# First two weight quads by plain block products, the whole beginning issued from one listed order

## The chip, the cores and the metric

One core of one Trainium2 chip runs the program. The metric is device microseconds of one execution, as the median of three runs. The engines of the core are called by the profile's names: PE (TensorE), DVE (VectorE), ACT (ScalarE), POOL (GpSimd) and SP (SyncE, which issues most of the DMAs). Each engine works through its own list of instructions in order and waits for others at semaphores.

## The reference

Three stages follow each other. An attention with pooled keys and values (4 batches, 8 heads, 576 tokens, head size 64), a mixture of 4 experts (512 to 1024 to 512, with a ReLU), and a gated second network behind a norm. The part around the change is the attention and the first of the experts:

```
k_p = k.reshape(B, H, Sp, 8, D).mean(axis=3)          # 576 -> 72 keys
v_p = v.reshape(B, H, Sp, 8, D).mean(axis=3)
attn = softmax(scale * q @ k_p.T)                     # with max subtracted, 1e-9 added to the sum
x = (attn @ v_p)                                      # 2304 tokens x 512
for e in range(4):
    h = maximum(x @ w1[e], 0)                         # 512 -> 1024
    out += p[:, e:e+1] * (h @ w2[e])                  # 1024 -> 512
```

## The kernel before

**Tiling.** The 2304 tokens are 18 tiles of 128. They are worked in three passes of 6 tiles; half A of a pass is its tiles 0 to 2, half B its tiles 3 to 5 (384 tokens each). Every fp32 operand of a product is split in a high and a low part (an fp32r copy by ACT, and the rest by DVE), and a product is three matmuls: high by high, high by low, low by high.

**Quads.** The first expert product of a pass goes quad by quad: a quad is a 512 by 256 block of `w1[e]`, cut in four blocks (B11, B22, B21, B12), each two times 128 rows deep. `quad` (line 441) computes the four outputs (two token halves by two column blocks) with seven block products instead of eight, after Strassen and Winograd (`STEPS`, line 43): it needs sums of the tokens of half A and half B (`s1` to `s4`), made by `x_ops` (line 117), and sums of the weight blocks (`tw`), made on POOL by `prep_w` (line 253). A step of `quad` is six matmuls of 384 columns. Four outputs of a quad, after the ReLU and again split, are `hA` and `hB`. Two quads together feed `second` (line 777), the product with `w2`: six token tiles (a tile is 12 matmuls of 512 columns into `py`), which are issued between the steps of the two quads that follow. Quads 0 and 1 have no such tiles beside them.

**The beginning.** Lines 1061 to 1133 load and pool keys and values of batches 0 and 1 (`pool_k` on DVE with copies by ACT, `pool_v` on POOL), run the attention of tiles 0 to 5 in the order 0, 3, 1, 4, 2, 5 (`att_sc` scores and row maximum, `att_ex` the exponentials on ACT, `att_b` the normalisation on DVE, `att_c` transposes to `tr` and copies to `aT`, `att_d` the product with the values `av` and the copy to `stg`), and put `x_ops` in between, once per pair of tiles (n and n + 3, whose sums it needs), for 128 columns at a time. The rule that sets the order is the loop of lines 1088 to 1122. `heat` (line 945) is a product that nobody reads. Only when all six tiles are through does quad 0 begin (line 1253). The attention of tiles 6 to 17 is spread over the steps of the quads by `when` (line 1139).

The tile pools give buffers out by tag; `hA` has 4 buffers, `hB` 3, `rw` and `tw` one each.

Of the kernel before, what the change touches and what calls it, by code (L numbers as in the profile page):

```python
# [11 lines left out]
F32 = mybir.dt.float32  # L12
# [38 lines left out]
)  # L51


@with_exitstack
def tile_kernel(ctx: ExitStack, tc, qp, kp, vp, dp, w1r, w2r, w64, rg, out):
# [61 lines left out]
    def x_ops(c0=0, c1=N, new=True):  # L117

        a11, a12, a21, a22 = (xr[o, d][:, :, c0:c1] for o in (0, N) for d in range(2))

        if new:
            for _, _, _, name in STEPS:
                new_xo(name)

        def high(name, src):
            nc.scalar.activation(xo[0][name][:, 0, :, c0:c1], src, AF.Copy)

        def low(name, src):
# [12 lines left out]
        low("s3", a21)
        add(a21, a22, ALU.add)
        high("a22", a22)
        yield
        add(a11, a21, ALU.add)
        high("s2", a21)
        high("a12", a12)
        yield
        low("s2", a21)
        low("a22", a22)  # L150
        high("s1", a11)
        yield
        low("a12", a12)
        low("s1", a11)
        add(a12, a21, ALU.subtract)
        yield
        high("s4", a12)
        yield
        low("s4", a12)
        yield  # L160
# [136 lines left out]

    raw2, w2 = {}, {}

    def load_w2(key):  # L300
        k, p, e, r = key
        if p:
            return
        t = main.tile([P, 2, DM], F32, name="rw2", tag="rw2")
        nc.sync.dma_start(t.rearrange("p s n -> p (s n)"), w2r[e, r])
        raw2[key] = t
# [17 lines left out]


# [115 lines left out]
    def quad(i, after):  # L441
# [8 lines left out]
        seeded = i > 0  # L450
# [29 lines left out]
    def new_h(half, key):  # L480
        t = late["sb"].tile([P, 2, 2, N], F32R, name="h" + half, tag="h" + half, bufs=4 if half == "A" else 3)
        h_t[half, key] = t
        return t

# [292 lines left out]
    def second(keys, first, last):  # L777

        k, p, e, _ = keys[0]
        for t in (3, 4, 5, 0, 1, 2):  # L780
# [12 lines left out]
            if first:  # L793
# [3 lines left out]
                nc.scalar.activation(y, ps, AF.Copy, scale=gate)  # L797
# [86 lines left out]
    def load_q(i):  # L884
# [8 lines left out]
        nc.sync.dma_start(t, qp[i].rearrange("p (j s) -> p j s", j=NPAIR))  # L893
# [9 lines left out]
    def pool_k(b, j, stage=None, eng=None):  # L903
# [9 lines left out]
        if eng is nc.vector:  # L913
            for i in range(2):
                c = at["sb"].tile([P, SP], F32, name="kc", tag="kc", bufs=2)
                nc.vector.tensor_reduce(c, stage[:, i], axis=AX.X, op=ALU.add)
                for hh in range(2):
                    sl = slice(64 * hh, 64 * hh + 64)
                    nc.scalar.activation(kpb[b % 2][sl, j + i, hh, :], c[sl], AF.Copy)
# [8 lines left out]
    def pool_v(b, h, stage=None, eng=None, queue=nc.sync):  # L928

        if stage is None:  # L930
            stage = at["sb"].tile([SP, 2 * POOL * D], F32, name="vr", tag="vr")
        else:
            stage = spare(stage)
# [4 lines left out]
        if eng is nc.vector:  # L938
            nc.vector.tensor_reduce(o, stage.rearrange("p h k d -> p h d k"), axis=AX.X, op=ALU.add)
# [4 lines left out]

    def heat(k):

        if "heat" not in at:
            at["heat"] = at["ps"].tile([P, 512], F32, name="heat")
        for _ in range(k):
            nc.tensor.matmul(at["heat"][:, :P], ident, ident, start=True, stop=True)  # L950

    def att_a(i):
        att_sc(i)
        att_ex(i)

    def att_sc(i):
# [5 lines left out]
        for j in range(NPAIR):  # L962
            o = (j % 2) * 2 * SP
            for p0, w, b in parts(i):
# [3 lines left out]
                )  # L968
        m = at["sb"].tile([P, H], F32, name="m", tag="m", bufs=2)
        sm = at["sb"].tile([P, H], F32, name="sm", tag="sm", bufs=2)  # L970
        es = at["sb"].tile([P, H, SP], F32, name="es", tag="es", bufs=2)
        v = sc[:, :, 0:4 * SP].rearrange("p a (h s) -> p a h s", h=4)
        scale = 1.0 / (POOL * math.sqrt(D))
        nc.vector.tensor_reduce(m.rearrange("p (a h) -> p a h", a=2), v, axis=AX.X, op=ALU.max)
        nc.vector.tensor_scalar(m, m, -scale, None, op0=ALU.mult)
        es_t[i] = es, sm, m, v, scale

    def att_ex(i):
        es, sm, m, v, scale = es_t[i]
        for h in range(H):  # L980
            nc.scalar.activation(
                es[:, h], v[:, h // 4, h % 4], AF.Exp, bias=m[:, h:h + 1], scale=scale, accum_out=sm[:, h:h + 1]
            )
        es_t[i] = es, sm

# [6 lines left out]
    def att_c(i):  # L992
        es, _ = es_t.pop(i)
        if i < TT:
# [4 lines left out]
        both = at["ps"].tile([P, 2, 512], F32, name="tr", tag="at") if at["few"] else None  # L999
        tr = [both[:, a] if at["few"] else at["ps"].tile([P, 512], F32, name="tr", tag="tr", bufs=3) for a in range(2)]  # L1000
        for h in range(H):
            nc.tensor.transpose(tr[h // 4][:SP, h % 4 * P:(h % 4 + 1) * P], es[:, h, :], ident)
        for a in range(2):
            src = tr[a][:SP, :].rearrange("p (h s) -> p h s", h=4)
            if a and not at["few"]:
                nc.vector.tensor_copy(aT[:, 4:], src)
            else:
                nc.scalar.activation(aT[:, 4 * a:4 * a + 4, :], src, AF.Copy)
        aT_t[i] = aT

    def att_d(i):
        aT = aT_t.pop(i)
        if at["few"]:
# [10 lines left out]
        avv = av.rearrange("p (j s) -> p j s", j=NPAIR)  # L1024
        p, t = divmod(i, TT)
        if p == 0:
            for d in range(2):
                nc.scalar.activation(
                    xr[t // HT * N, d][:, :, t % HT * P:t % HT * P + P], avv[:, 2 * d:2 * d + 2], AF.Copy,
                    scale=1.0 / POOL,  # L1030
                )
# [308 lines left out]
```

## Time and profile before

| | |
|---|---|
| median of three runs | 1278.03 us (1276.87 to 1280.02) |
| the profiled execution | 1276.43 us |
| its span, first to last instruction | 1274.1 us |
| PE busy share of the span | 98% |
| DVE, ACT, POOL busy share | 65%, 42%, 21% |
| mean granted TensorE clock | 0.992 of full speed |

The span is what the trace covers; the 2.3 us between it and the profiled execution's time lie outside the trace. A busy PE row counts the products that nobody reads too, and the matmuls at a reduced clock.

### The profile page before, as it was taken

Reading aid. Unit: us, or ns where it says so; the run is one execution under the profiler, and the core shown is the slowest. Engines: PE = TensorE matmul, PEld = TensorE weight load, DVE = VectorE, ACT = ScalarE, POOL = GpSimd, SP = SyncE. Lnnn points to the kernel's source line nnn. Section 1 sums busy time; section 2 is a strip of 40 time slices with the busy share of each in tenths; the row PEclk is TensorE's granted clock in tenths of the full one; section 3 lists DMA queues with packets and bytes.
Section 4 is the critical chain, followed back from the end, with each engine's and each line's share of the span. In section 5 each row is a group of like instructions: output and inputs, shape, how many; then the busy total and the mean of one; then the engine's idle time right before and its main releaser. Section 6 shows DMA issues by size and latency. Waiting matters only on the chain.

```text
span 1274.1 us, 18396 instructions
## 1 busy us (share of the span) xinstructions
PE 1247.5 (98%) x6872; PEld 1153.5 (91%) x6872; DVE 828.2 (65%) x1340; ACT 535.4 (42%) x1239; POOL 268.7 (21%) x253
## 2 busy tenths in 40 slices
PE   7899999999999999999999999999999999999998
PEld 6788888888988888888889998888999999999998
DVE  5864556557466676645677787475667765786575
ACT  5674444444453333323443333255454433433331
POOL 5335333410031222200242343122220000000000
PEclk8899999999999999999999999999999999999999
DMA  8297777768788786664989998747877776867671
GB/s 248 85 340 278 276 252 248 286 236 313 277 309 281 258 286 255 233 246 168 330 312 332 325 326 314 281 177 274 328 263 277 279 293 254 313 242 295 233 275 50
DMA packets 118937, 339.15 MB, mean 266 GB/s; under 512 B 10304, under 2 KB 48192, under 8 KB 99648
## 3 DMA queue, kind: packets, MB, share of 16 engines
q1 hardware_dynamic: 118512, 336.80, 73.0%
q10 hardware_dynamic: 336, 1.18, 0.3%
q8 instruction: 54, 0.88, 0.3%
q14 instruction: 35, 0.29, 0.1%
HBM read 233.61 MB, written 104.33 MB: 265 GB/s over the span
## 4 chain that ended last, share of the span: by engine, by line
PE 84%; DVE 8%; DMA 4%; ACT 2%; issue 1%; SPq 0%; DVEq 0%; ACTq 0%
PE py L788 9%; PE py L789 9%; PE py L787 9%; PE qX L462 8%; PE qX L464 8%; PE qX L463 8%; PE qY L462 4%; PE qY L463 4%; PE qY L464 4%; PE qZ L462 2%; PE qZ L464 2%; PE qZ L463 2%; DMA wc_d<-cx 2%; PE gy L734 1%; PE gx L667 1%; PE av L1020 1%
## 5 line engine op out<-in xcount | busy, mean ns | idle before, releaser
L799 DVE SCALAR_TENSOR_TENSOR y<-py,dps,y 128x512 f32<-128x512 f32 x126 | 94.4, 749 | 186.4 <-PE py L789 186.3
L377 POOL TENSOR_TENSOR cx<-cx 128x512 f32<-128x512 f32 x36 | 49.8, 1383 | 380.4 <-DVE cx L376 91.2
L462 PE MATMUL qX<-xos,wt 128*128 128x384 f32 x336 | 116.2, 346 | 5.1 <-ACT s L470 3.5
L464 PE MATMUL qX<-xos,wt 128*128 128x384 f32 x336 | 113.6, 338 | 0.0
L789 PE MATMUL py<-w,hB 128*128 128x512 f32 x288 | 113.5, 394 | 0.0
L789 PE MATMUL py<-w,hA 128*128 128x512 f32 x288 | 113.4, 394 | 0.0
L788 PE MATMUL py<-w,hB 128*128 128x512 f32 x288 | 113.3, 393 | 0.0
L788 PE MATMUL py<-w,hA 128*128 128x512 f32 x288 | 113.2, 393 | 0.0
L463 PE MATMUL qX<-xos,wt 128*128 128x384 f32 x336 | 113.1, 337 | 0.0
L787 PE MATMUL py<-w,hB 128*128 128x512 f32 x288 | 112.0, 389 | 0.0
L787 PE MATMUL py<-w,hA 128*128 128x512 f32 x288 | 112.0, 389 | 0.0
L491 ACT ACTIVATE hB<-u 128x768 fp32r<-128x768 f32 x48 | 40.8, 850 | 139.3 <-DVE u L474 139.2
L273 POOL TENSOR_TENSOR tw<-rw 128x512 f32<-128x512 f32 x28 | 41.3, 1474 | 263.0 <-DVE wt L291 192.0
L470 ACT ACTIVATE s<-qX 128x384 f32<-128x384 f32 x85 | 41.6, 490 | 120.3 <-PE qX L464 120.2
L467 ACT ACTIVATE qZ<-qX 128x384 f32<-128x384 f32 x83 | 39.8, 480 | 120.5 <-PE qX L464 82.6
L472 DVE TENSOR_TENSOR u<-qY,s 128x384 f32<-128x384 f32 x84 | 46.5, 553 | 56.5 <-PE qY L464 27.2
L462 PEld LDWEIGHTS qX<-xos,wt 128*128 128x128 f32 x336 | 63.3, 188 | 13.2 <-ACT s L470 5.8
L463 PEld LDWEIGHTS qX<-xos,wt 128*128 128x128 f32 x336 | 63.3, 189 | 2.9
L789 PEld LDWEIGHTS py<-w,hB 128*128 128x128 f32 x288 | 54.0, 188 | 11.5
L789 PEld LDWEIGHTS py<-w,hA 128*128 128x128 f32 x288 | 54.0, 188 | 11.4
L464 PEld LDWEIGHTS qX<-xos,wt 128*128 128x128 f32 x336 | 63.1, 188 | 0.2 <-DVE wt L291 0.2
L788 PEld LDWEIGHTS py<-w,hA 128*128 128x128 f32 x288 | 54.0, 188 | 10.1
(188 smaller groups left out, 3499.4 us busy)
## 6 DMA issues: line engine op xcount, KB each, us to landing
wt<-wt_d SPq DMA_DIRECT2D x56, 1024.0 KB, 7.4
w<-w_d SPq DMA_DIRECT2D x32, 1024.0 KB, 8.6
wt_d<-wt SPq DMA_DIRECT2D x28, 1024.0 KB, 7.3
wr<-wr_d SPq DMA_DIRECT2D x56, 512.0 KB, 8.0
wr_d<-wr SPq DMA_DIRECT2D x28, 768.0 KB, 5.9
cr<-w SPq DMA_DIRECT2D x36, 512.0 KB, 7.1
w<-ws_d SPq DMA_DIRECT2D x18, 1024.0 KB, 5.8
w_d<-w SPq DMA_DIRECT2D x16, 1024.0 KB, 9.0
```

What stands on the lines that cost most here:

```text
L273: nc.gpsimd.tensor_tensor(t[:, T1:N3 + 1], r[:, B12:B12 + 1].to_broadcast([P, 2, 256]), r[:, B11:B22 + 1], op=sub)
L377: nc.gpsimd.tensor_tensor(x, x, m.bitcast(F32), op=ALU.mult)
L462: nc.tensor.matmul(bank[b], wh, xh, start=first and k == 0, stop=False, **kw)
L463: nc.tensor.matmul(bank[b], wh, xl, start=False, stop=False, **kw)
L464: nc.tensor.matmul(bank[b], wl, xh, start=False, stop=k == 1, **kw)
L470: nc.scalar.activation(s[n], bank[b], AF.Copy)
L472: nc.vector.tensor_tensor(u[:, 0], bank["Y"], s[2], op=ALU.add)
L491: nc.scalar.activation(h[:, 0], u, AF.Relu)
L787: nc.tensor.matmul(ps, lhs[0], w[:, 0, c], start=j == 0, stop=False)
L788: nc.tensor.matmul(ps, lhs[0], w[:, 1, c], start=False, stop=False)
L789: nc.tensor.matmul(ps, lhs[1], w[:, 0, c], start=False, stop=j == len(units) - 1)
L799: nc.vector.scalar_tensor_tensor(y_t[t], ps, gate, y_t[t], op0=ALU.mult, op1=ALU.add)
```

## The change

The beginning, up to the start of quad 2, becomes a table `ORDER` of some 280 single steps, each a small function, called in the listed order. Attention goes in tile order 0 to 5. The raw attention result of half A (tiles 0 to 2) is split at once, and quads 0 and 1 are computed for half A from it by plain block products (`by_half`: for one half and one column block, 12 matmuls into one accumulator), then for half B; so each of the two quads has 48 matmuls of 384 columns instead of 42, and needs no token sums and no weight sums (these are still made in the table: the token sums for quad 2, the weight sums because later passes read them back). Five of the six `second` tiles of quads 0 and 1 stand in the table as well (`y0` to `y4`), and the sixth goes beside quad 3. Three of the four value loads of batch 0 are pooled by PE (8 accumulated products with the identity) and not by POOL; the pooled keys of batch 1 are copied by POOL and not by ACT. Block B12 of quads 0 and 1 gets its own split (`wb`). The first two query loads go out on ACT's queue, the value loads on SP's. The later attention tiles of pass 1 are spread at every 13th step and not at every 16th, since two quads fewer are left to spread them over.

```diff
+ORDER = """
+Lq0 heat24 Lk0a Lq1 k0a ow0 Lk0b k0b Lv0a or0 sc0 Lw0 Lv0b ws0 v0a xo mx0 ex0 Lv0d sc1 t00 v0d Lq2 wh0 Lv0c
...
+"""
...
+    def by_half(i, h, c):
+        w = wop[i]
+        key = quads[i]
+        o = h_t.get(("AB"[h], key)) if c else new_h("AB"[h], key)
+        ps = late["ps"].tile([P, 512], F32, name="qX", tag="qX", bufs=2)[:, :N]
+        blocks = ((B11, B21), (B12, B22))[c]
+        for j, (name, slot) in enumerate(zip((("a11", "a12"), ("a21", "a22"))[h], blocks)):
+            for k in range(2):
+                sl = slice(k * P, (k + 1) * P)
+                wh, wl = (w["b"][a][:, sl] if slot == B12 else w["r"][:, a, slot, sl] for a in range(2))
+                xh, xl = (xo[0][name][:, a, k] for a in range(2))
+                nc.tensor.matmul(ps, wh, xh, start=j == k == 0, stop=False)
+                nc.tensor.matmul(ps, wh, xl, start=False, stop=False)
+                nc.tensor.matmul(ps, wl, xh, start=False, stop=j == k == 1)
+        def out(j):
+            if j:
+                nc.vector.scalar_tensor_tensor(
+                    o[:, 1, c], ps, 0.0, f32(o[:, 0, c]), op0=ALU.max, op1=ALU.subtract
+                )
+            else:
+                nc.scalar.activation(o[:, 0, c], ps, AF.Relu)
...
-        seeded = i > 0
+        seeded = i > 2
...
+                    if b:
+                        nc.gpsimd.tensor_copy(o, c[sl])
+                    else:
+                        nc.scalar.activation(o, c[sl], AF.Copy)
...
+            for k in range(POOL):
+                nc.tensor.matmul(t, ident[:SP, :SP], stage[:, :, k], start=k == 0, stop=k == POOL - 1)
...
+    v0 = [pool_v(0, h, t, e) for h, t, e in (
+        (0, "hA", nc.tensor), (2, "hB", nc.tensor), (4, "hB", nc.tensor), (6, None, None)
+    )]
...
+    py = second(pair, True, False, range(TT), late_y)
...
-    for n in range(TT + 2):
-        if n < TT:
-            att_ex(order[n])
...
+    for name in ORDER.split():
+        do[name]()
+    at["few"] = 1
...
-        return (p - 1) * NSTEP + 2 + 16 * t
+        return NSTEP - 12 + 16 * t if p > 1 else 2 + 13 * t
...
-        for i in ids:
+        for i in ids[2 * (si == 0):]:
```

What the steps are called: `Lq`, `Lk`, `Lv`, `Lw`, `Lx` are loads; `sc`, `mx`, `ex`, `nm`, `tr`, `ca`/`cd`, `av`, `rw` are one attention tile's scores, maximum, exponentials, normalisation, transposes, two copies, value product and raw copy; `ha`/`hd` and `l` its high and low parts; `pihc` is the product of quad i, half h, column block c, and `r`, `s` its ReLU high and low part; `wh`, `wl`, `ws`, `t` prepare a quad's weights, `xh`, `xl` a row of `w2`; `y`, `o` a `second` tile and its copy out.

The order on PE around the first quad product. Before, the rows that end the attention of the last tile and open quad 0 (`xoa` and `xos` are the split tokens and token sums, `tr` transposes, `av` the value product):

```order
L950 MATMUL heat<-ident 128x128 x10
L1002 MATMUL tr<-ident,es 72x128 x8
L1020 MATMUL av<-aT,vpb_90 64x128 x8
L1020 MATMUL av<-aT,vpb_93 64x128 x8
L950 MATMUL heat<-ident 128x128 x4
L462 MATMUL qX<-xoa_385,wr 128x384
```

In the changed kernel, the same engine from the third tile's transposes on (`vs` is a value sum on PE, line 1042; lines 558 to 560 are `by_half`):

```order
L1042 MATMUL vs<-stg,ident 72x128 x8
L1120 MATMUL tr<-ident,es 72x128 x8
L1154 MATMUL av<-aT,vpb_90 64x128 x8
L1120 MATMUL tr<-ident,es 72x128 x8
L1154 MATMUL av<-aT,vpb_90 64x128 x16
L1076 MATMUL sc<-kpb_88,y 128x144 x4
L558 MATMUL qX<-xoa_175,wr 128x384
```

Before, six tiles' transposes and value products stand ahead of the first quad product; now those of three tiles, and the scores of a fourth.

The same on ACT. Before, from the exponentials of the first two tiles on (line 981 `es` is one head's exponentials, eight to a tile; line 1028 the raw copies of a tile, line 126 the high parts):

```order
L981 ACTIVATE es,sm<-sc,m 128x72 x16
L919 ACTIVATE kpb_91<-kc 64x72 x8
L1008 ACTIVATE aT<-tr 72x512
L981 ACTIVATE es,sm<-sc,m 128x72 x8
L1008 ACTIVATE aT<-tr 72x512
L1028 ACTIVATE stg<-av 128x2x128 x2
```

In the changed kernel, the same place:

```order
L1094 ACTIVATE es,sm<-sc,m 128x72 x8
L331 ACTIVATE wt<-tw 128x512
L1094 ACTIVATE es,sm<-sc,m 128x72 x16
L1130 ACTIVATE aT<-tr 72x512
L1049 ACTIVATE vpb_90<-vs 72x384
L1130 ACTIVATE aT<-tr 72x512
L1171 ACTIVATE stg<-av 128x4x128
L1180 ACTIVATE xoa_175<-stg 128x2x128
```

The eight key copies of batch 1 (`kpb_91`) are gone from ACT's list, three tiles' exponentials stand back to back but for one weight part, and a tile's raw copy is one instruction and is followed by its high part.

On SP, the loads. Before, after the first query tile (`kp` keys, `vp` values, `w1r` and `w2r` weights):

```order
L911 DMA stg<-kp 128x576 x4
L893 DMA y<-qp 128x512 x2
L911 DMA kr<-kp 128x576 x2
L911 DMA stg<-kp 128x576 x2
L893 DMA y<-qp 128x512 x3
L250 DMA rw<-w1r 128x1024
L305 DMA rw_150<-w2r 128x1024
```

In the changed kernel, from the start (its second `vr<-vp` reuses the buffer of the first, and waits until POOL has pooled that):

```order
L1004 DMA stg<-kp 128x576 x4
L1034 DMA stg<-vp 72x1024
L240 DMA rw<-w1r 128x1024
L1034 DMA stg<-vp 72x1024
L1034 DMA vr<-vp 72x1024
L986 DMA y<-qp 128x512
L352 DMA stg<-w2r 128x1024
L1034 DMA vr<-vp 72x1024
L1004 DMA kr<-kp 128x576 x2
```

The weights of quad 0 moved ahead of most values and of the keys of batch 1, and a load that waits for POOL stands ahead of those keys.

## Rows read from the trace of the kernel before

**Rows 1.** The page's head: the span and PE's busy share.

```profile
span 1274.1 us, 18396 instructions
PE 1247.5 (98%) x6872; PEld 1153.5 (91%) x6872; DVE 828.2 (65%) x1340; ACT 535.4 (42%) x1239; POOL 268.7 (21%) x253
```

**Rows 2.** Busy time by stretch: engines in order, granted clock, DMA share, GB/s.

```profile
12.00:54.08 42.08, 34.75 (x314) 31.35 (x314) 33.12 (x65) 29.85 (x140) 18.68 (x21) 0.87 0.51 157
54.08:66.32 12.24, 11.75 (x50) 10.34 (x51) 10.33 (x22) 7.77 (x29) 3.49 (x3) 0.75 0.36 107
66.32:77.76 11.44, 8.65 (x52) 8.04 (x51) 10.35 (x16) 8.40 (x17) 3.34 (x3) 1.00 0.79 296
77.76:95.58 17.82, 17.82 (x104) 15.84 (x103) 10.05 (x16) 11.54 (x34) 6.32 (x7) 1.00 1.03 404
...
10.00:20.00 10.00, 8.11 (x34) 7.18 (x35) 6.87 (x11) 6.46 (x39) 5.93 (x8) 0.54 1.03 330
...
55.00:60.00 5.00, 4.95 (x14) 4.26 (x15) 4.39 (x12) 3.10 (x8) 0.34 (x1) 0.50 0.00 0
```

**Rows 3.** Whom PE waited for up to 77.7 us: total, times, longest.

```profile
PE tr L1002 <- DVE es L990: 4.0, 2, 2.4
...
PE qX L462 <- ACT xoa L126: 2.3, 1, 2.3
...
PE qX L462 <- ACT qZ L467: 1.2, 1, 1.2
```

**Rows 4.** PE in order of time: start, duration, line, instruction, count.

```profile
31.65 1.25 PE L965 MATMUL sc<-kpb,y 128*128 128x144 f32 x8
32.74 2.39 PE L950 MATMUL heat<-ident 128*128 128x128 f32 x20
34.98 1.04 PE L1002 MATMUL tr<-ident,es 128*72 128x128 f32 x8
35.95 1.09 PE L1020 MATMUL av<-aT,vpb 72*64 72x128 f32 x16
...
54.08 0.69 PE L462 MATMUL qX<-xoa,wr 128*128 128x384 f32 x1 [2.28 <-ACT xoa L126]
...
77.76 0.33 PE L462 MATMUL qX<-xoa,wr 128*128 128x384 f32 x1
...
78.80 0.33 PE L462 MATMUL qY<-xos,wt 128*128 128x384 f32 x1
...
85.90 0.39 PE L787 MATMUL py<-w,hB 128*128 128x512 f32 x1
...
88.67 0.33 PE L462 MATMUL qX<-xos,wt 128*128 128x384 f32 x1
...
112.10 0.33 PE L462 MATMUL qX<-xoa,wr 128*128 128x384 f32 x1
```

**Rows 5.** ACT in order of time: first head of the first and of the second tile.

```profile
13.66 0.32 ACT L981 ACTIVATE es<-sc,m 128x72 f32<-128x72 f32 x1 [2.00 <-DVE m L975]
...
16.05 0.36 ACT L981 ACTIVATE es<-sc,m 128x72 f32<-128x72 f32 x1
```

**Rows 6.** DVE in order of time: a maximum, one normalisation beside POOL's work and one alone.

```profile
12.60 0.76 DVE L974 TENSOR_REDUCE m<-sc 128x8 f32<-128x576 f32 x1 [1.51 <-PE sc L965]
...
33.29 1.54 DVE L990 TENSOR_TENSOR es<-es,sm 128x576 f32<-128x576 f32 x1
...
40.49 0.16 DVE L988 TENSOR_SCALAR sm<-sm 128x8 f32<-128x8 f32 x1
...
40.92 0.76 DVE L990 TENSOR_TENSOR es<-es,sm 128x576 f32<-128x576 f32 x1
41.60 0.42 DVE L130 TENSOR_TENSOR xoa<-stg,xoa 128x256 fp32r<-128x256 f32 x1
```

**Rows 7.** Groups by line and shape, 0 to 112 us: count, busy us, mean ns, idle before.

```profile
L1008 ACT ACTIVATE aT<-tr 72x512 f32<-72x512 f32 x10 | 5.7, 593 | 3.4 <-PE tr L1002 3.3
L126 ACT ACTIVATE xoa<-stg 128x256 fp32r<-128x256 f32 x9 | 3.7, 411 | 0.0
L990 DVE TENSOR_TENSOR es<-es,sm 128x576 f32<-128x576 f32 x8 | 8.5, 1059 | 0.3
L925 POOL TENSOR_TENSOR kpb<-kr 64x144 f32<-64x144 f32 x4 | 3.0, 754 | 0.3
```

More of the change, by code (lines that the diff above doesn't have):

```diff
@@ L323, in prep_w2, with w2_part, w2_put @@
         put(d, tf)
+    def w2_part(key, c, j):
+        if key not in w2:
+            w2[key] = main.tile([P, 2, 2, DM], F32R, name="w2", tag="w2", bufs=4)
+        t, r = w2[key], raw2[key]
+        if j:
+            nc.vector.tensor_tensor(t[:, 1, c], r[:, c], f32(t[:, 0, c]), op=ALU.subtract)
+        else:
+            nc.scalar.activation(t[:, 0, c], r[:, c], AF.Copy)
+        if c and j:
+            raw2.pop(key)
+    def w2_put(key):
+        nc.sync.dma_start(w2_d[key[2] * R1 + key[3]], f32(w2[key]).rearrange("p a s n -> p (a s n)"))
     def convert_all():
@@ L775, in new_y, with second @@
         return late["sb"].tile([P, HT * DM], F32, name="y", tag=f"y{half}")
-    def second(keys, first, last):
+    def second(keys, first, last, tiles=(3, 4, 5, 0, 1, 2), later=None):
         k, p, e, _ = keys[0]
-        for t in (3, 4, 5, 0, 1, 2):
+        for t in tiles:
             half, sl = "AB"[t // HT], slice(t % HT * P, t % HT * P + P)
@@ L954, in att_a @@
         att_ex(i)
+    SCALE = 1.0 / (POOL * math.sqrt(D))
     def att_sc(i):
@@ L998, in att_c, with att_ca, att_cd, att_av @@
             aT = at["sb"].tile([SP, H, P], F32, name="aT", tag="aT")
[L999 to L1013, printed above, removed]
+        aT_t[i] = aT, [t[:SP, :].rearrange("p (h s) -> p h s", h=4) for t in tr]
+    def att_ca(i, a=0):
+        aT, tr = aT_t[i]
+        nc.scalar.activation(aT[:, 4 * a:4 * a + 4, :], tr[a], AF.Copy)
+        tr[a] = None
+    def att_cd(i):
+        aT, tr = aT_t[i]
+        nc.vector.tensor_copy(aT[:, 4:], tr[1])
+        tr[1] = None
+    def att_c(i):
+        att_tr(i)
+        att_ca(i)
+        att_ca(i, 1)
+    def att_av(i):
+        aT, _ = aT_t.pop(i)
+        if at["few"] == 2:
+            av = late["ps"].tile([P, 512], F32, name="av", tag="qY")
+        elif at["few"]:
             av = at["ps"].tile([P, 2, 512], F32, name="av", tag="at")[:, 0]
@@ L1123, in tile_kernel @@
-    heat(4)
-    run(xit, 30)
-    for _ in wit:
-        pass
-    nc.sync.dma_start(dps, dp)
-    gates()
-    nc.sync.dma_start(g_bc, rg.to_broadcast([P, DM]))
-    psa.release()
-    late["ps"] = tc.alloc_tile_pool(name="psl", bufs=1, space=bass.MemoryType.PSUM)
-    at["ps"] = tc.alloc_tile_pool(name="psb", bufs=1, space=bass.MemoryType.PSUM)
-    at["few"] = True
+                if one:
+                    break
+    rows = [q for q in quads if q[0] == "m"]
+    side = []
+    pair = [quads[0], quads[1]]
@@ L1136, in tile_kernel @@
+    step("Lw3", load_w, 3)
+    for n in range(5):
+        step(f"y{n}", py_tile)
+        step(f"o{n}", lambda: late_y.pop(0)())
+    for name in ("s3", "s2", "s1", "s4"):
+        step("add" + name, x_sum, name)
+        step("hi" + name, x_part, name, 0)
+        step("lo" + name, x_part, name, 1)
+    for k in range(1, 30):
+        step(f"heat{k}", heat, k)
+    for name in ORDER.split():
+        do[name]()
+    at["few"] = 1
+    xit = []
     NSTEP = 7 * E * R1
@@ L1166, in att_close @@
         late["pg"] = tc.alloc_tile_pool(name="psg", bufs=1, space=bass.MemoryType.PSUM)
-    side = []
     bg, norms = [], []
@@ L1176, in tile_kernel @@
         stages[-1][1].append(i)
-    def row_of(i):
-        k, p, e, r = quads[i]
-        return (k, p, e, r) if k == "m" else None
-    rows = [row_of(i) for i in range(NQ) if row_of(i)]
-    nrow = [0]
+    nrow = [2]
     def prep_row():
```

340 lines of the change are left out of this document (213 added, 127 removed).

## The prediction, made before the changed kernel had run

> **What bounds the kernel now.** I read the page's head first: PE is busy for 98% of the span [rows 1], so nearly everywhere the time is the sum of PE's work, and there is nothing to gain but where PE does useless work or none. The table of stretches shows where that is [rows 2]. From 77.76 us on PE is busy without a gap. In the 42.08 us before quad 0 (12.00 to 54.08) it is busy for 34.75, but that contains the products that nobody reads: the heat groups and the attention at half clock. The list of waits names the causes [rows 3]: PE waited for the normalised exponentials (DVE) and for the split tokens (ACT), so before 54 us the chain through ACT and DVE sets the time. In quad 0 (54.08 to 66.32) the granted clock is 0.75, and in quad 1 PE works only 8.65 of 11.44 us. In PE's timeline, quad 0 starts at 54.08, quad 2 at 77.76 and quad 4 at 112.10 [rows 4]. So the question is when the changed kernel reaches a place where both have done the same work. I take the first product of quad 4: from there on both lists on PE are the same, but for the places of the attention tiles.
>
> **Unit prices.** On PE six matmuls of 384 columns are one step: 78.80 - 77.76 = 1.04 us; a `second` tile is 88.67 - 85.90 = 2.77; scores 1.25, transposes 1.04, value product 1.09, heat 2.39 for 20 records [rows 4]. On ACT a tile's exponentials take 16.05 - 13.66 = 2.39 [rows 5]. On DVE a maximum with its scaling is 0.9 (0.76 by itself, 1.06 from its start to the first exponential at 13.66 [rows 5, 6]), a normalisation 41.60 - 40.49 = 1.11 where POOL rests [rows 6]. A copy of 512 elements on ACT is 0.59, a split part of 256 is 0.41 on either engine [rows 5 to 7], which I use for the new 128x256 casts on DVE too: no row shows one, it can cost nothing or 0.42, and six of them, spread, move the sum by under a microsecond.
>
> **What goes, what comes.** The plain products cost 2 x 6 more matmuls, 2 x 1.04 = 2.1 us of PE. Pooling three value loads on PE costs 3 x 16 records at 2.39/20 = 0.12, so 1.9 us each; no trace shows this product, but the heat records have the same shape and I take their price (twice that at half clock). It lies ahead of the second and third maximum, so only the last part of it can show. The seven token operands in three column pieces, with which quad 0's first product had to wait for all six tiles, go from the path.
>
> **The walk through the new order.** E is the end of the third tile's exponentials. The keys of batch 0 come first in both kernels, so the first exponential starts at 13.66 again. Three tiles and one weight part: 3 x 2.39 + 0.6 = 7.8, E = 21.4. If PE stays at half clock, as it did from 10 to 20 us (0.54 granted [rows 2]), one value pooling and two scores ahead of the second maximum run double and the second tile's exponentials start about 3 us late: E = 24.5. The longer heat at the start speaks for the early end, the row for the late one; I take 22.5.
>
> From E to the first quad product: two copies 1.2, then on PE in turn value product 1.1, transposes 1.0, two value products 2.2, then the third tile's raw copy 0.6, its high part 0.4, two low parts 0.8: 7.3. Quad 0's first product starts at about 30, not 54.
>
> From there to the first `second` tile the longest chain is: maximum 0.9, exponentials of tile 3 2.4, ReLU parts ahead of the normalisation 1.0, normalisation 1.1, two key reductions 1.5 (as a maximum, 0.76 each), the four key copies now on POOL 1.9, then PE, which meanwhile does transposes and values of tile 3 and is 0.8 late, scores 1.25, maximum 0.9, exponentials 2.4, the quad product ahead 0.9, scores 1.25, transposes 1.0, copies and a value product of two batches 2.4: 19.8. The copies on POOL have no row; a 64x144 sum takes 0.75 there [rows 7] and a 64x72 copy is half of that, so I take 0.47; at nothing the chain is 0.8 us shorter (PE is then the later one), at 0.75 it is 1.1 longer. The first `second` tile starts at E + 27.1.
>
> From there PE is the bound: five `second` tiles 13.9, transposes 1.0 and values 1.1 of tile 5, four products of 2.08 for half B, 8.3: 24.3. Beside it DVE has some 13 us of work after tile 5's raw copy (token sums, low parts, weights of quad 2), which must fit in about 16; it does, without much room. Quad 2 starts at E + 51.4.
>
> POOL and DVE now work beside each other for most of this. The normalisation's last part takes 0.76 alone and 1.54 while POOL pools, 1.06 on average [rows 6, 7]: six tiles lose 6 x 0.3 = 1.8, other instructions some; I add 2.5. Quad 2 at 22.5 + 51.4 + 2.5 = 76.4.
>
> Quads 2 and 3 have one `second` tile and one attention tile beside them: 14 steps 14.6, tile 2.8, attention 1.25 + 1.04 + 1.09 = 3.4: 20.8. Quads 0 and 1 before show what happens when so little stands between: the wait for ACT's copy `qZ` (1.2, [rows 3]) comes again in quad 3, and some of the wait for the normalisation, together 1.5. The other new wait is on ACT: quad 3's `hB` needs a buffer that the sixth `second` tile of quads 0 and 1 still reads; behind it on ACT stand weight parts and `hA`, for which PE waits only in the next quad. Nothing of it reaches PE as long as that tile lies ahead of the last step. Quad 4 starts at 76.4 + 22.3 = 98.7.
>
> Before, it starts at 112.10, but there the next attention tile's scores and transposes were done (about 2 us): 110.1. The gain is 11.4 us, the span 1274.1 - 11.4 = 1262.7, the execution with the 2.3 us outside the trace 1265.0. The profiled execution lies 1.6 us under the median of its three runs, well inside the 0.3% (3.8 us) that such runs can tell from no change; I predict **1265**.
>
> **Loads.** SP issues in order, and its second load into `vr` waits until POOL has pooled the first, behind the weight sums of quad 0. From 10 to 20 us the DMAs are full (1.03, 330 GB/s [rows 2]), so what is ahead of that load (4.4 MB) keeps them busy to about 16 us, when POOL is through; then 2.3 MB of values, queries and keys of batch 1 come by about 25, and are wanted at E + 8.2 = 31. That is 6 us of slack.
>
> **The rivals.**
> *Given back in quads 2 and 3* (chance 0.20). Each quad writes its split weights back and loads the next, about 3.9 MB; at the 404 GB/s of quads 2 and 3 before [rows 2] that is 9.6 us, and the quads now want 10.4 each. If they take quad 1's 11.44 each and the tile and the rest of the attention on top (2.8 + 2.3), 28.0 in place of 22.3, the time is 1271. For it: quad 1 of before; against it: there POOL's and DVE's backlog of the attention stood behind it.
>
> *DVE becomes the bound* (0.12). From the first product to quad 2 the table gives DVE, at these prices, about 34 us of work in 44. If POOL stretches a third of it as it did at 33.29 (1.54 for 0.76), 34/3 = 11 us come on top and half of it shows: 1270. On page SBUF — State Buffer, section Who interferes with whom, the Trainium skill says that a VectorE instruction with two SBUF inputs and a GpSimd one that reads SBUF exclude each other for a whole instruction, and that casts can do so as well; the two normalisation rows agree, and by that rule the new casts would be stretched too.
>
> *Better than the sum* (0.13). Clock up from the start, no extra stretch, no stall in quads 2 and 3: 21.4 + 51.4 + 20.8 = 93.6, gain 16.5: 1260.
>
> *The table is held by a load* (0.03): the first weights land late, POOL is late, the keys of batch 1 beyond their 6 us; each further microsecond counts in full. At 10 us late: 1269.
>
> *The clock, on the slower side* (0.05). After 2.28 us without work ahead of quad 0, PE ran at 0.50 from 55 to 60 [rows 2, 4]; the table drops most heat groups. If PE falls there and stays at 1.2 GHz through the PE-bound part, its 24.3 us double: 24.3 - 11.4 = 13 us slower, 1289. It decides from 11.4 us of lost PE work on, half of that part. Against it: in the new order no wait of PE between E and quad 2 comes out over 1.5 us, and 20 to 40 us ran at full clock. On page TensorE: Matmul & The Clock Gate, section Part 1, the Trainium skill says that the slow state is the default and sustained activity lifts it; the row agrees, and by it this part, which has hardly a gap, would run at full clock.
>
> The forecast itself holds 0.47; its own range, from E's two ends, POOL's copies and the stretch, is 1261 to 1270.
>
> **How the numbers follow.** The range 1257 to 1273 takes in the first three rivals and leaves out the clock and the far ends of the others. Faster by over 0.3% (under 1274.2) is the forecast, the first three rivals and the held load but for their tails: 0.88; within 0.3%: 0.07; slower: 0.05.
>
> **What would show it.** Right: the first plain product near 30 us, the first `second` tile near 50, quad 2 near 76, quad 4 near 99, a clock of 1.0 from about 20 us on, and everything after shifted by the same 11 us. Wrong: quad 2 in time but quad 4 after 103 (given back); DVE without idle time from 30 to 76 (DVE bound); a clock under 0.9 between 50 and 76; a PE wait of several microseconds on a POOL copy or on a DMA before the fifth tile's scores.

## The result, and the profile after

The changed kernel takes 1266.44 us (median of four runs, 1266.2 to 1268.74) against 1279.03 for the kernel before beside it: a ratio of 0.9907, with a 95% interval of 0.9886 to 0.9927. 1265.0 was predicted, with 1257 to 1273 as the range. The profiled execution took 1266.2 us, its span is 1264.4 (before 1276.43 and 1274.1). The traces therefore show 9.7 us of the 12.6 between the medians; the profiled execution of the kernel before was faster than all four of its timed runs here.

The steps of the walk, each from PE's timeline or ACT's:

| step | predicted | measured |
|---|---|---|
| first exponential | 13.66 | 12.33 |
| E, third tile's exponentials end | 22.5 | 20.5 |
| E to the first quad product | 7.3 | 6.8 |
| from there to the first `second` tile | 19.8 | 19.8 |
| from there to quad 2 | 24.3, and 2.5 for stretched instructions | 24.8 |
| quads 2 and 3 | 22.3 | 25.5 |
| quad 4 starts | 98.7 | 97.34 |
| from quad 4 to the end of the span | 1164.0 | 1167.1 |

The page's head, with PE at 98% as in [rows 1]:

```profile
span 1264.4 us, 18367 instructions
PE 1242.1 (98%) x6876; PEld 1149.0 (91%) x6876; DVE 833.4 (66%) x1335; ACT 529.3 (42%) x1211; POOL 264.6 (21%) x252
```

PE's timeline at the crossing places (the third row is the value product of the sixth tile, the fifth the transposes of tile 6, for which PE waits in quad 3):

```profile
27.27 0.43 PE L558 MATMUL qX<-xoa,wr 128*128 128x384 f32 x1
...
47.06 0.50 PE L874 MATMUL py<-w,hA 128*128 128x512 f32 x1
...
54.08 1.09 PE L1154 MATMUL av<-aT,vpb 72*64 72x128 f32 x16
...
71.86 0.33 PE L523 MATMUL qX<-xoa,wr 128*128 128x384 f32 x1
...
86.84 0.71 PE L1120 MATMUL tr<-ident,es 128*72 128x128 f32 x5 [2.11 <-DVE es L1108]
...
97.34 0.44 PE L523 MATMUL qX<-xoa,wr 128*128 128x384 f32 x1
```

The sixth tile's value product ends at 55.2. Before, the last one ended at 50.7, and quad 0 began at 54.08 [rows 4]:

```profile
48.74 1.97 PE L1020 MATMUL av<-aT,vpb 72*64 72x128 f32 x32
```

So the attention is not faster at all, but slower; by its end PE has half A of two quads and two `second` tiles behind it.

The table of stretches (the first as in [rows 2], then the steps of the walk, then the two 5-us stretches around the wait):

```profile
10.00:20.00 10.00, 8.83 (x75) 8.17 (x75) 8.90 (x15) 7.62 (x47) 5.77 (x6) 1.00 0.77 213
27.27:47.06 19.79, 18.41 (x164) 16.69 (x162) 15.78 (x31) 12.22 (x50) 13.86 (x20) 1.00 0.19 62
47.06:71.86 24.80, 24.64 (x137) 21.07 (x133) 20.18 (x33) 14.37 (x35) 6.50 (x6) 1.00 0.79 285
71.86:97.34 25.48, 22.39 (x129) 20.82 (x127) 17.52 (x28) 16.69 (x43) 7.48 (x7) 0.93 0.93 347
85.00:90.00 5.00, 3.16 (x16) 3.19 (x17) 3.33 (x5) 0.82 (x3) 2.12 (x3) 0.80 0.95 324
90.00:95.00 5.00, 5.00 (x23) 4.53 (x23) 2.13 (x5) 2.56 (x6) 0.00 (x0) 0.86 1.01 399
```

From 27 to 72 us PE is busy for 43.05 of 44.59 us, at a granted clock of 1.00. In quads 2 and 3 it waits, and then runs partly at the lower level (0.50): at a mean of 0.93, 0.07 x 25.48 = 1.8 us are lost.

Whom PE waited for from 80 us on:

```profile
PE tr L1120 <- DVE es L1108: 2.1, 1, 2.1
PE qX L523 <- ACT qZ L528: 1.0, 1, 1.0
```

DVE's timeline says why. Tile 6's exponentials were done at 79.9, but its normalisation (L1106 to L1108) stands in DVE's list behind other work of quads 2 and 3, of which the last three instructions are shown:

```profile
82.98 0.68 DVE L368 TENSOR_TENSOR w<-rw,w 128x512 fp32r<-128x512 f32 x1
83.59 0.55 DVE L588 SCALAR_TENSOR_TENSOR hA<-s,hA 128x384 fp32r<-128x384 f32 x1
84.06 0.55 DVE L588 SCALAR_TENSOR_TENSOR hA<-qX,hA 128x384 fp32r<-128x384 f32 x1
84.52 0.79 DVE L1106 TENSOR_SCALAR sm<-sm 128x8 f32<-128x8 f32 x1
85.34 0.20 DVE L1107 RECIPROCAL sm<-sm 128x8 f32<-128x8 f32 x1
85.58 1.12 DVE L1108 TENSOR_TENSOR es<-es,sm 128x576 f32<-128x576 f32 x1
```

Behind quad 4 the lead shrinks. It is 112.10 - 97.34 = 14.76 there, less 2.06 us for the attention parts that only the kernel before had done (scores and transposes, by their starts in [rows 4]), so 12.7; at the end of the span it is 1274.1 - 1264.4 = 9.7. The lines of PE's list of waits from quad 4 to the end that differ, first in the changed kernel, then in the one before:

```profile
PE qX L523 <- ACT s L531: 4.5, 5, 1.9
PE qX L523 <- DVE u L535: 2.0, 4, 1.0
PE qX L523 <- ACT qZ L528: 0.9, 3, 0.6
PE qY L523 <- DMA wt<-wt_d: 0.6, 1, 0.6
```

```profile
PE qX L462 <- ACT s L470: 3.5, 5, 1.2
PE qX L462 <- DVE u L474: 1.4, 4, 0.6
PE qX L462 <- ACT qZ L467: 0.4, 2, 0.2
```

With the other lines, the same in both lists (2.0 us), the waits are 10.0 and 7.3 us: 2.7 of the 3 us.

### The profile page after: what moved, and what is told of

It reads as the page before. It is cut to its first block, busy times and chain, and to the rows that moved or that the text cites. A ratio compares the mean times of both kernels' runs of the same rounds, so it can differ in the third digit from the quotient of the medians.

```text
span 1264.4 us, 18367 instructions
## 1 busy us (share of the span) xinstructions
PE 1242.1 (98%) x6876; PEld 1149.0 (91%) x6876; DVE 833.4 (66%) x1335; ACT 529.3 (42%) x1211; POOL 264.6 (21%) x252
## 4 chain that ended last, share of the span: by engine, by line
PE 83%; DVE 8%; DMA 4%; ACT 3%; issue 1%; POOL 0%; SPq 0%; ACTq 0%; DVEq 0%; POOLq 0%
PE py L876 9%; PE py L875 9%; PE py L874 9%; PE qX L523 8%; PE qX L525 8%; PE qX L524 8%; PE qY L523 4%; PE qY L525 4%; PE qY L524 4%; PE qZ L523 2%; PE qZ L525 2%; PE qZ L524 2%; DMA wt<-wt_d 1%; PE gy L821 1%; DMA wc_d<-cx 1%; PE gy L823 1%
## 5 line engine op out<-in xcount | busy, mean ns | idle before, releaser
L523 PE MATMUL qX<-xos,wt 128*128 128x384 f32 x328 | 113.6, 346 | 6.5 <-ACT s L531 4.5
L525 PE MATMUL qX<-xos,wt 128*128 128x384 f32 x328 | 111.2, 339 | 0.0
L524 PE MATMUL qX<-xos,wt 128*128 128x384 f32 x328 | 110.8, 338 | 0.0
L263 POOL TENSOR_TENSOR tw<-rw 128x512 f32<-128x512 f32 x25 | 36.8, 1474 | 222.4 <-DVE wt L281 168.9
L523 PEld LDWEIGHTS qX<-xos,wt 128*128 128x128 f32 x328 | 61.9, 189 | 14.3 <-ACT s L531 6.2
L524 PEld LDWEIGHTS qX<-xos,wt 128*128 128x128 f32 x328 | 61.9, 189 | 2.7
L876 PEld LDWEIGHTS py<-w,hA 128*128 128x128 f32 x288 | 54.0, 188 | 11.4
L874 PEld LDWEIGHTS py<-w,hA 128*128 128x128 f32 x288 | 54.2, 188 | 10.1 <-issue 0.2
L875 PEld LDWEIGHTS py<-w,hA 128*128 128x128 f32 x288 | 54.0, 188 | 10.2 <-DVE w L378 0.3
```

Of the source, the lines that this page charges most:

```text
L523: nc.tensor.matmul(bank[b], wh, xh, start=first and k == 0, stop=False, **kw)
L524: nc.tensor.matmul(bank[b], wh, xl, start=False, stop=False, **kw)
L525: nc.tensor.matmul(bank[b], wl, xh, start=False, stop=k == 1, **kw)
L874: nc.tensor.matmul(ps, lhs[0], w[:, 0, c], start=j == 0, stop=False)
L875: nc.tensor.matmul(ps, lhs[0], w[:, 1, c], start=False, stop=False)
L876: nc.tensor.matmul(ps, lhs[1], w[:, 0, c], start=False, stop=j == len(units) - 1)
```

## The experiments

Theory A is the prediction's: the attention of six tiles is a chain through ACT, DVE and POOL, and the gain is the work that PE does beside it. The rivals: earlier keys and the clock (B, N), PE as the bound everywhere (C), and for single pieces that a wait only changes its name. "Quad 2" and "quad 4" are the starts of these quads in PE's timeline. For comparison, the changed kernel: first exponential 12.33, first product 27.27, first `second` tile 47.06, quad 2 71.86, quad 4 97.34, 1266.4 us.

**late_half**: half A behind the whole attention.

```diff
-... p000 ... p001 ... r000 ... s000 ... p100 ... r001 ... p101 ... nm5 y0 tr5 ... y1 ca5 l04 o0 cd5 av5
+... nm5 tr5 ... ca5 l04 cd5 av5 p000 r000 s000 p001 r001 s001 p100 r100 s100 p101 r101 s101 y0 y1 o0
```

> The half A products of quads 0 and 1 and the first two second tiles move behind the attention of all six tiles; the plain products, the loads and everything else stay. Theory A (the gain is that PE works on half A while the softmax of tiles 3 to 5 runs on ACT and DVE): the attention of tile 5 would end near 49 us, and 8.3 us of half A products, 13.9 of second tiles and 8.3 of half B products follow it, 30.5 in all: quad 2 near 79.5 instead of 71.86, the time 7 to 8 us above the changed kernel, about 1274. Theory B (the gain is the earlier keys, the shorter attention and the clock, and the products fit in anywhere): quad 2 within 2 us of 71.86, about 1267.

Measured: 1281.43 us, ratio to before 1.0018 (1.0005 to 1.0031). First product 55.41, quad 2 88.28, quad 4 112.19. All of the gain is gone; the loss of 15.0 us is twice what theory A said. PE's timeline shows two things: PE waits for the softmax of single tiles, and most of this stretch runs at half clock (0.50 to 0.52 from 35 to 45 and from 50 to 60 us).

```profile
43.61 2.29 PE L1076 MATMUL sc<-kpb,y 128*128 128x144 f32 x8 [4.05 <-ACT es L1094]
...
51.68 1.89 PE L1120 MATMUL tr<-ident,es 128*72 128x128 f32 x8 [2.97 <-DVE es L1108]
53.50 1.98 PE L1154 MATMUL av<-aT,vpb 72*64 72x128 f32 x16
55.41 0.69 PE L558 MATMUL qX<-xoa,wr 128*128 128x384 f32 x1
```

**late_warm**: the same, with PE kept busy in its waits.

```diff
-... sc3 ... heat12 ... sc5 ... tr5
+... sc3 ... heat24 ... heat17 sc5 ... heat13 tr5
```

> As late_half, with products nobody reads (24, 17 and 13 instead of 12, by place) in the waits of 2.9, 4.1 and 3.0 us that PE had there in front of tile 3's transposes, tile 5's scores and tile 5's transposes. Theory A with the clock as a second cause (late_half lost 7 to 8 us of overlap, and the rest of its 15 because PE ran at half clock from 33 to 61 us): the granted clock is 1.00 throughout, the first quad product near 51 instead of 55.41, quad 2 near 81 instead of 88.28, the time 1273 to 1276. Theory G (the products behind the attention cost 15 us by themselves, the clock is a by-product): quad 2 stays above 86 and the time above 1279.

Measured: 1278.60 us, ratio 1.0000 (0.9984 to 1.0016); first product 56.31, quad 2 86.90, quad 4 111.24. The clock was 0.98 from 45 to 60 us (0.50 only from 40 to 45), and the first product came no earlier. The second cause that I had added to theory A explains little: 1.4 us at quad 2. Nor is G's number clean, since the added products, part of them at half clock, cost some time themselves. From the first product 30.5 us of PE work follow, and 56.3 + 30.5 = 86.8: that sum holds. What was wrong was the start; I had put the end of the attention near 49 and it lies at 55 to 56, in the changed kernel, in late_half and in late_warm.

**before_warm**: the clock alone, in the kernel before.

```diff
-    heat(12)
+    heat(24)
...
-    heat(4)
+    heat(13)
```

> The kernel before, with twice the products nobody reads at its start (heat of 24, not 12) and more of them in PE's wait ahead of quad 0 (13, not 4), so that PE does not rest there. Theory N (a good part of the change's gain is the clock, 0.50 from 10 to 15 us and from 55 to 60): the granted clock is 1.00 in these stretches, quad 4 starts 3 to 5 us earlier than 112.10, the time about 1274. Theory A (before, quads 0 and 1 wait for ACT and DVE, and the attention ahead of them is their chain; a faster PE waits longer): the clock rises, quad 4 within 2 us of 112.10, the time 1277 to 1279.

Measured: 1280.46 us, ratio 1.0016 (1.0003 to 1.0029), quad 4 at 113.18 instead of 112.10. The clock rose in both stretches that theory N names, against 0.54 and 0.50 in [rows 2]; there PE's busy time fell from 8.11 to 6.55 and from 4.95 to 2.67, and little came of it: the last tile's exponentials started 1.35 earlier (40.21), its normalisation ended at 47.86 instead of 47.62, and from quad 0 to quad 4 both kernels take 58.0 us. Even the 1.35, had nothing taken it back, is well under the 3 to 5 us of theory N; N falls. The 1.1 us at quad 0 (55.15 for 54.08) are the variant's own: from 45 to 50 us its clock was lower (0.67, before 0.84), and the unread products of that stretch held the last transposes up to 48.84.

```profile
10.00:20.00 10.00, 6.55 (x47) 5.16 (x48) 7.47 (x13) 7.20 (x41) 6.11 (x8) 1.00 1.01 324
...
45.00:50.00 5.00, 5.00 (x32) 4.81 (x34) 2.76 (x7) 1.81 (x6) 0.00 (x0) 0.67 0.39 106
...
55.00:60.00 5.00, 2.67 (x13) 2.10 (x13) 4.42 (x13) 3.13 (x10) 0.00 (x0) 1.00 0.00 1
```

**no_heat**: the group between the first two products left out.

```diff
-... l12 p000 heat12 mx3 k1a p001 ...
+... l12 p000 mx3 k1a p001 ...
```

> The heat group between the first two half A products (24 records, 2.6 us on PE at 29.45) is left out. Theory A (there PE waits for softmax and keys anyway, and the clock does not need the group): the first second tile stays within 0.7 us of 47.06, the clock 1.00, the time within 1 us of 1266.4. Theory C (PE is the bound from the first product on): 2.6 us faster, 1264. Theory D (the clock needs it): granted clock under 0.9 somewhere between 30 and 50 us and the time 2 us or more above 1266.4.

Measured: 1267.14 us (1263.36 to 1268.25), ratio 0.9893 (0.987 to 0.9917). First `second` tile 48.86, 1.8 us later and not earlier, and from 30 to 40 us PE is busy for 5.86 of 10 us: PE is not the bound there, and C falls, although the times alone (down to 0.987) would allow its 1264. Behind that PE runs through a stretch at 0.66: D by its clock, but the time is only 0.7 us above the changed kernel's and within its scatter. The 1.8 us are scatter in part as well: early_norm, which does the same as the changed kernel up to there, has this tile at 48.04.

```profile
40.00:45.00 5.00, 5.00 (x22) 5.00 (x21) 4.79 (x11) 2.54 (x16) 4.20 (x6) 0.66 0.00 0
```

**short_heat**: half the group at the start.

```diff
-Lq0 heat24 Lk0a ...
+Lq0 heat12 Lk0a ...
```

> The heat group at the start has half the matmuls (12 instead of 24), so PE rests about 4 us before the first scores. Theory A (the prediction's late bound: at half clock the value pooling and the scores ahead of the second and third maximum take twice as long): granted clock near 0.5 somewhere between 9 and 20 us, the first quad product 1.5 to 3 us later than 27.27, and the time up to 3 us above 1266.4. Theory F (the clock stays up, or what PE does there hides behind the exponentials): the first quad product within 0.5 us of 27.27, 1266.

Measured: 1268.00 us, ratio 0.9909 (0.9889 to 0.9929); first product 29.29, 2.0 later, although the first exponential came at 11.46; quad 4 at 98.81. Theory A's late bound is real in the trace; the times of the two kernels overlap:

```profile
10.00:15.00 5.00, 5.00 (x24) 5.00 (x24) 3.21 (x4) 3.04 (x17) 3.61 (x4) 0.50 0.90 224
```

**pool_values**: POOL pools all values of batch 0.

```diff
-        (0, "hA", nc.tensor), (2, "hB", nc.tensor), (4, "hB", nc.tensor), (6, None, None)
+        (0, "hA", None), (2, "hB", None), (4, "hB", None), (6, None, None)
```

> All four value blocks of batch 0 are pooled by POOL, as in the kernel before, and none by PE; the copy of PE's sums to the values is gone too. Theory A: POOL has the weight sums until 14.0 and then four blocks of 2.5 to 2.9 us, so the values are complete near 25 instead of 21; the first value product waits from 21.5 to about 25, the first quad product comes near 31 and the time is 3 to 4 us above, 1270. Theory J (as A, and PE, without 5.7 us of pooling in 10 to 20 us, falls to half clock): granted clock under 0.9 between 10 and 30 us, first quad product at 33 or later, 1272 or more. Theory K (PE's pooling costs as much as it saves): 1266.4 within 1 us.

Measured: 1274.69 us, ratio 0.9966 (0.9954 to 0.9978); first product 35.61, quad 4 106.51: theory J. PE waited 3.0 us for POOL, nearly as A said, and most of the rest goes with the clock, 0.50 from 15 to 35 us: from the third tile's transposes to the first product the same work takes 8.1 us (27.47 to 35.61), in the changed kernel 4.7 (22.56 to 27.27). Two of PE's waits, then two stretches:

```profile
PE sc L1076 <- ACT es L1094: 3.3, 1, 3.3
PE av L1154 <- POOL vpb L1045: 3.0, 1, 3.0
```

```profile
15.00:20.00 5.00, 4.04 (x17) 3.42 (x18) 4.29 (x10) 3.92 (x23) 4.69 (x6) 0.50 0.35 124
...
30.00:35.00 5.00, 4.30 (x35) 3.90 (x32) 2.73 (x6) 2.93 (x6) 1.27 (x1) 0.50 0.62 193
```

**loads_back**: the queues of the first loads as before.

```diff
-        step(f"Lq{i}", load_q, i, nc.scalar if i < 2 else nc.sync)
+        step(f"Lq{i}", load_q, i, nc.sync)
...
-    v0 = [pool_v(0, h, t, e) for h, t, e in (
+    v0 = [pool_v(0, h, t, e, nc.scalar) for h, t, e in (
```

> The first loads go out as in the kernel before: the query tiles on SP ahead of and among the keys, the value blocks of batch 0 on ACT's queue; the rest as in the changed kernel. Theory A (the earlier start of the first exponential, 12.33 for 13.66, is the load order's, and everything behind it is one chain up to the first quad product): first exponential 13.4 to 13.9, first quad product 28.4 to 29, the time 1.3 us above, about 1267.7. Theory I (the start hides behind something later): the first exponential later, the first quad product within 0.4 us of 27.27, 1266.4.

Measured: 1272.80 us, ratio 0.9958 (0.9942 to 0.9973); first exponential 12.52, first product 34.61, quad 4 103.72. Neither theory: the keys were hardly later. On ACT's queue the value loads go out only when ACT gets there: the first two at 9.06 and 9.72, behind copies of the keys (2.60 and 3.87 in the changed kernel), the last two behind exponentials, at 13.26 and 13.65. In the kernel before they went out at 0.87 to 6.98, so this is no clean return. The first pooling waited for its block, and the clock fell to 0.50 and 0.53 from 15 to 25 us.

```profile
13.63 2.94 PE L1042 MATMUL vs<-stg,ident 72*72 72x128 f32 x16 [2.68 <-DMA stg<-vp]
16.36 2.13 PE L1076 MATMUL sc<-kpb,y 128*128 128x144 f32 x8
18.28 3.62 PE L1042 MATMUL vs<-stg,ident 72*72 72x128 f32 x16
```

**early_norm**: tile 6's normalisation two steps earlier.

```diff
-        for o, f in ((0, att_a), (4, att_b), (7, att_c), (11, att_d)):
+        for o, f in ((0, att_a), (2 if i == TT else 4, att_b), (7, att_c), (11, att_d)):
```

> The normalisation of the first later attention tile (tile 6) is issued two steps earlier, so that DVE has it behind the exponentials that end at 79.7 and not behind quad 3's other work at 84.52. Theory A (quads 2 and 3 lose 2.1 us to that wait, and 1.8 us to the half clock that follows it): quad 4 starts 3 to 4 us earlier than 97.34, the time about 1263. Theory E (quad 3 is bound by DVE and ACT together, and one wait is replaced by the next): quad 4 within 1 us of 97.34, the clock still falls, 1266.

Measured: 1262.73 us, ratio 0.9862 (0.9839 to 0.9884), 3.7 us below the changed kernel. Quad 2 started 1.0 later in this profile (72.86) and quad 4 2.15 earlier (95.19), so quads 2 and 3 took 22.3 us instead of 25.5: 2.1 of the wait and 1.8 of the clock, less 0.6, because the wait for `qZ` grew from 1.0 to 1.6. E falls.

```profile
72.86:95.19 22.33, 20.68 (x129) 19.34 (x127) 16.69 (x27) 16.21 (x43) 7.89 (x6) 1.00 0.87 321
```

**keys_first**: early_norm, and POOL copies the keys of batch 1 ahead of two value blocks.

```diff
-... Lv1b v1b l11 ... mx3 k1a p001 xl01 ex3 r000 or1 s000 xh00 nm3 tr3 v1a wh1 k1b ...
+... Lv1b l11 ... mx3 k1a k1b p001 xl01 ex3 r000 or1 s000 xh00 nm3 tr3 v1b v1a wh1 ...
```

> early_norm, and POOL gets the eight key copies of batch 1 ahead of the poolings of two value blocks (2.7 us each) and not behind them; DVE's second pair of key reductions moves up too. Theory A (the tile whose scores use batch 1's keys waits for POOL, 0.6 us in the changed kernel and 1.3 in early_norm, and that wait stands on the chain to the first second tile): no wait of PE for these copies, the first second tile 1 to 1.5 us earlier than early_norm's 48.04, the time about 1261.5. Theory H (the chain is held by softmax on ACT and DVE as much as by the keys, or the value blocks come late instead): within 0.5 us of early_norm, 1262.7.

Measured: 1261.04 us, ratio 0.9864 (0.9846 to 0.9882), the lowest time of the study, but by its ratio level with early_norm (0.9862). PE's wait for these copies, 0.6 in the changed kernel and 1.3 in early_norm, is gone; that is theory A's. What it is worth is less clear: the first `second` tile came at 46.73, 1.3 before early_norm's but 0.3 before the changed kernel's, and these two do the same up to there. Quad 4 started at 93.89. POOL's timeline in the changed kernel shows what stood ahead of the copies (L991 and L1045 pool values); its first row waits for a load, which landed 1.3 us later in early_norm (30.25):

```profile
28.96 2.41 POOL L991 TENSOR_TENSOR stg<-stg 72x512 f32<-72x512 f32 x2 [11.93 <-DMA stg<-vp]
...
31.85 1.56 POOL L1014 COPY kpb<-kc 64x72 f32<-64x72 f32 x4
33.49 2.08 POOL L991 TENSOR_TENSOR stg<-stg 72x512 f32<-72x512 f32 x2
35.64 1.87 POOL L1045 TENSOR_TENSOR vpb<-stg 72x128 f32<-72x128 f32 x1
37.46 1.11 POOL L1014 COPY kpb<-kc 64x72 f32<-64x72 f32 x4
```

**early_row**: keys_first, and quad 2's row of `w2` split from the first step on.

```diff
-                if n >= 2:
+                if n >= 2 or i == 2:
```

> keys_first, and in quad 2 the splitting of a row of w2 (two copies of 0.6 us on ACT, two subtractions on DVE) starts at the first step and not at the third, so that it is not left over behind quad 2. Theory A (PE's wait of 1.7 us in quad 3 for ACT's copy qZ is ACT's backlog from quad 2): that wait falls to about 1.0, quad 4 0.6 us earlier, the time 0.6 lower, about 1260.4. Theory M (ACT there waits for DVE and PE, not for its own backlog): the wait stays within 0.3 of 1.7.

Measured: 1262.04 us, ratio 0.9866 (0.9841 to 0.9891), the wait 1.8: theory M. ACT stood idle ahead of the copies in question, for DVE, which now has the normalisation at this place (81.33 to 82.53):

```profile
83.03 0.52 ACT L583 ACTIVATE hA<-s 128x384 fp32r<-128x384 f32 x1 [1.09 <-DVE s L538]
83.46 0.47 ACT L586 ACTIVATE hA<-qX 128x384 fp32r<-128x384 f32 x1
83.83 0.48 ACT L528 ACTIVATE qZ<-qX 128x384 f32<-128x384 f32 x1
```

**old_offsets**: keys_first, and the later tiles' transposes and value products at their old distance.

```diff
-... (7, att_c), (11, att_d)):
+... (8, att_c), (13, att_d)):
```

> keys_first, and the transposes and the value product of every later attention tile go back to 8 and 13 steps behind its scores (7 and 11 in the changed kernel). Background weight conversion on DVE goes only into steps that hold no attention part, so this moves it too. Theory A (part of the waits after quad 4, 7.3 us before and 8.5 to 10.2 in the changed kernel and its variants, comes from where the conversion now falls: the wait of 0.57 us 296 us behind quad 4 stands in every variant and not before): that wait goes, the span behind quad 4 falls from 1165.7 to 1164 to 1165, the time about 1260. Theory L (the waits after quad 4 are chance): the 0.57 stays, the time within 1 us of 1261.

Measured: 1269.42 us, ratio 0.9921 (0.99 to 0.9941), 8.4 us above keys_first, and 6.7 between the profiled spans. The wait of 0.57 us, 296 us behind quad 4, is gone, as theory A said, but with tiles every 13 steps a value product 13 steps behind the scores meets the next tile's scores: PE waits four times for ACT to copy the value product out (4.3 us) and once more for 0.7, and from 200 to 250 us the clock is 0.97, 1.5 us more: together 6.5 us.

```profile
PE sc L1076 <- ACT st L1166: 4.3, 4, 2.2
```

**both**: old_offsets and early_row.

> old_offsets and early_row together. If both theories A hold, the two gains add: about 1259.5; if neither, 1261.

Measured: 1270.36 us, ratio 0.9925 (0.9901 to 0.9948): old_offsets again, and nothing from early_row.

## Why the prediction was right, step by step

**The bound: right.** PE is busy for 98% of the span [rows 1], and yet what bound the beginning was the softmax chain: before_warm gave PE its clock back from 10 to 20 and from 55 to 60 us and gained nothing, late_half and late_warm put the products behind the chain and lost all of the gain. In the changed kernel and in these two the last value product ends at 55.2 to 56.4 us; in the kernel before and in before_warm it ends earlier, at 50.7 and 51.8, so the gain is not a shorter chain.

**E: 2.0 early, for a reason that the walk denied.** "The keys of batch 0 come first in both kernels, so the first exponential starts at 13.66 again" failed: the first key sum starts at 3.88 and not at 6.63, in the changed kernel and in the one before:

```profile
3.88 0.75 DVE L1009 TENSOR_REDUCE kc<-stg 128x72 f32<-128x576 f32 x1 [3.88 <-DMA stg<-kp]
...
6.63 0.75 DVE L916 TENSOR_REDUCE kc<-stg 128x72 f32<-128x576 f32 x1 [6.63 <-DMA stg<-kp]
```

What had held it was rather the value blocks that were loaded beside the keys than the query ahead of them, since loads_back, which has the query ahead again and the values later, starts it at 4.26. At the first exponential 1.3 of these 2.7 us were left; among other things a scaling of 128x8 ahead of it took 1.18. How much the start counts is doubtful: seven profiles with the same order on PE up to the first product (the changed kernel, no_heat and the five runs from early_norm on) have the first exponential at 11.21 to 12.33 and the first product at 27.02 to 27.44 all the same. The other side of E, half clock, did not happen (1.00 from 10 to 20 us), but the term was sized well: short_heat has it, at 2.0 us on the first product, where the walk had 3.

**The pooling of values on PE: size right, part of its worth missed.** 16 records were priced at 1.9 and took 1.91. The prediction counted them as a cost that hides. pool_values is 8.3 us slower: 3.0 are POOL's lateness, and most of the rest goes with the clock, which was at 0.50 from 15 us on where this work was missing.

**From the first product to quad 2: right, the first part of it by luck.** 19.8 for 19.8 and 24.8 for 24.3. Within the 19.8 two errors cancel: the fifth tile's exponentials started 12.9 us after the first product (40.18), where the terms of the walk give 11.8, and what followed took 6.9 and not 8.0. The copies on POOL were priced at 0.47 (half of the 0.75 that the walk names would be 0.38) and took 0.28 to 0.39, but the walk left out that value blocks stand ahead of them on POOL, 4.0 us of pooling ahead of the last four; this is the wait that keys_first took out. The rival of the held load came true in small there, by a value block of batch 1, pooled ahead of the key copies, that landed only at 28.96. DVE was not the bound: it was busy for 36.0 of these 44.6 us (34 by the walk), and PE for 43.05. Six of the new casts cost 0.29 each.

**The allowance of 2.5 for POOL and DVE beside each other: not needed.** Instructions were stretched: the last part of a normalisation took 1.04 at 15.68, during POOL's pooling, and 0.76 at 18.44, where POOL rested; one of the new casts took 0.81 at 12.62, during POOL's weight sums. The Trainium skill, page SBUF — State Buffer, section Who interferes with whom, says that a VectorE instruction with two SBUF inputs contends with a GpSimd one that reads SBUF, and that casts can contend as well; these rows agree. PE had other work at these places.

**Quads 2 and 3: the step that was off by 3.2.** The wait for `qZ` and "some of the wait for the normalisation, together 1.5" was 1.0 for `qZ`, 2.1 for the normalisation and 1.8 for the clock that fell behind that wait. Part of the rival "given back in quads 2 and 3" came true (25.5, between 22.3 and its 28.0), but not by its mechanism: early_norm moved the three DVE instructions of one normalisation ahead of six others, left the transfers alone, and got 22.3.

**Behind quad 4: a step that the walk left out.** That everything after would be "shifted by the same 11 us" failed: 12.7 became 9.7. Of the 2.7 us of longer waits, 0.57 is understood in part. At 383 and 384 us DVE has two pieces of background weight conversion (1.32 and 1.52) ahead of a tile's maximum; such conversion goes only into steps without attention, and these fall elsewhere now; moving the attention's steps took the wait away (old_offsets). The other waits vary between runs of kernels that don't differ there (the wait that was longest in the changed kernel, 1.9 ahead of 617.62, was 0.8 in early_norm and keys_first and 2.4 in early_row); whether the rest of the loss is chance or the new spacing stays open.

**The sum.** The walk was 1.4 us pessimistic up to quad 4 (E and the allowance against quads 2 and 3) and 3.1 optimistic behind it: 1265.0 for 1266.4 is partly luck. The gain from trace to trace was 9.7 us, where the walk had 11.4. The clock on the slower side did not come true as priced, but pool_values and loads_back show that it was near: waits of PE of 2.7 us up to 13.63 (loads_back) and 3.3 us up to 15.07 (pool_values), with what followed them, cost 6 to 8.

## What to carry to other kernels

If PE looks full at the start of a kernel, look at whether it is full of work that counts: the chain of softmax steps got no shorter here by a faster PE (before_warm), but a product that needs only half of its results fitted beside it, even at a price of 2 us of plain matmuls.
When work is moved, follow each in-order list past the place where it lands: here a normalisation behind six DVE instructions cost 3.9 us with the clock, and key copies behind a value block on POOL a wait of 0.6 to 1.3.
A spacing and the distances inside it belong together: with 13 steps between tiles, a value product 13 steps behind the scores (and transposes 8) cost 8 us against 11 (and 7).

## What the runs showed of the hardware

- Scaling a 128x8 tile on DVE takes 0.17 us at 17.43 and took 1.18 at 11.05, while POOL's weight sum ran (10.95 to 12.21); for the second tile it took 1.20 at 14.13, while POOL pooled values (14.04 to 16.10).
- After a rest of 2.1 us ahead of 86.84 the granted clock was 0.80 and 0.86 in the next two stretches of 5 us, though PE worked for all of the second; another rest, of 0.98 us, had ended at 83.40. In keys_first, after a single rest of 1.66 us ahead of 83.77, it stayed at 1.00 (85 to 95 us).
- In pool_values the granted clock stayed at the lower level (0.50) from 15 to 35 us, with PE busy for 2.9 to 4.3 of each 5 us.
- Leaving out 2.6 us of products that nobody reads (no_heat) made nothing faster: the clock was 0.66 from 40 to 45 us where it is 1.00 with them, and the first `second` tile came at 48.86, with them at 47.06 and, in early_norm, at 48.04.
